# Starting the first batch by halves of its heads in a one-core attention and snake kernel

## The chip, the cores and the metric

One core of one Trainium2 chip runs the whole program. The metric is the device time of one execution in microseconds (us). Where the granted TensorE clock of an execution was below 0.997 of full speed, the text says so. PE is TensorE, ACT ScalarE, DVE VectorE, POOL GpSimd, SP SyncE.

## The reference

Attention without a score matrix, then a two-layer block with the snake activation. Eight batches, eight heads, 576 positions, 64 columns per head.

```python
q_s = softmax(q, over head_dim)            # exp, sum, divide
k_s = softmax(k, over seq)
kv  = einsum('bhsd,bhse->bhde', k_s, v)
x   = einsum('bhsd,bhde->bhse', q_s, kv)   # -> 4608 tokens x 512
h   = x @ w_in                             # 512 -> 2048
g   = h + sin(alpha * h)**2 / alpha
out = g @ w_out                            # 2048 -> 512
```

## The kernel before

Tokens go through the two products in nine rows of 512. A row has 16 blocks of h (128 of the 2048 columns each): four matmuls over the four k-chunks of x give a block, ACT takes its sine, one of ACT, DVE and POOL squares it, DVE combines (`g = h + s / alpha`), and PE multiplies g by w_out into four accumulators. Row t = 0 can't start until the first batch's q, k, v have been loaded, exponentiated, normalised and multiplied into x. "Half 0" and "half 1" below are the two halves of the heads: half 0 gives x chunks 0 and 1, half 1 gives chunks 2 and 3.

The kernel has eight PSUM banks at hand, and until the end of row 1 they are split in two pools:

```python
ps_h = tile_pool(name="ps_h", bufs=4, space=PSUM)      # single banks
ps_e = tile_pool(name="ps_e", bufs=2, space=PSUM)      # double banks, lent to h
...
def mm_h(t, ni, wide=None, k0=0, k1=4):                # one block of h
    ...
    elif wide and ni % 6 in ((2, 3) if t == 0 else (4, 5)):
        hp = wide()                                    # a lent buffer (named hh)
    else:
        hp = ps_h.tile([128, MF], F32, name="hp", tag="h")
    for ki in range(k0, k1):
        nc.tensor.matmul(hp, win[:, ki, ...], xT[:, ki, ...], start=(ki == 0), stop=(ki == 3))
```

The start, with GpSimd issuing the loads of v and of the weights, and all four x chunks made after both halves of kv:

```python
GP_CP(held, staged["q", 0][:, 0, 0, 0:1])              # waits for q, holds the issues below
for ii, j0, j1 in ((0, 0, 9), (1, 0, 5), (1, 5, 9)):
    GP.dma_start(... v ...)
for c0, c1 in ((0, 256), (256, 512), (512, 1024), (1024, 1536), (1536, 2048)):
    load_win(c0, c1)                                   # two transfers each, all four k-chunks
...
for ii in range(2):
    kv_mm(0, ii, ps_e, split=True)
    kv_norm(0, ii, ii + 1)
for c in range(4):
    xp = ps_h.tile([128, MF], F32, name="hp", tag="h")
    attn_chunk(0, c, 0, 8, xp)
    (ACT_CP, DVE_CP)[c % 2](xT[:, c, 0:MF], xp)
```

Row 0 and the start of its second product:

```python
for ni in range(nN):
    h_slot(0, ni, "DPAPPAPPAPPAPPAP"[ni], lag, lent)   # who squares: DVE, POOL, ACT
    flush(lag, 1)                                      # combine, one block behind
    if ni in late: late[ni]()
flush(lag, 0)
accs = [ps_h.tile([128, dm], F32, name="hp", tag="h") for _ in range(4)]
os = o_quad(0, accs, ...)                              # the first 8 alternate accumulators 0 and 1
take(os, 20)                                           # 20 of the 64 matmuls
```

The softmax here doesn't subtract the row's maximum and nothing guards it: scores larger than these inputs give would overflow.

## Time and profile before

| | before |
|---|---|
| median (3 runs) | 288.67 us (288.63 to 289.37) |
| span of the profiled run | 286.8 us |
| first q landed, its exp starts | 4.94 us |
| h stream of row 0 starts | 15.74 us |
| first sine | 17.73 us |
| combine of block 13 ends | 31.66 us |
| tenth o matmul | 31.72 us |
| h stream of row 1 starts | 47.23 us |

The prediction below shows the lines that carry its reading. The first is the stretch-by-stretch table, one microsecond each: stretch, length, then busy time and count for PE, PE's weight loads, DVE, ACT and POOL, then the granted clock, the share of the DMA engines, and GB/s.

### The profile page before, as it was taken

The numbers are of one execution on the slowest core, as the hardware profiler recorded it, in microseconds if no ns is written. First come the engines' busy times: TensorE is split into PE (matmuls) and PEld (weight loads), VectorE is DVE, ScalarE is ACT, GpSimd is POOL, SyncE is SP. The second block draws the span as 40 slices with busy tenths as digits, with TensorE's granted clock in tenths as the row PEclk, the third lists the DMA queues.
The fourth block names the chain that finished last, engine by engine and source line by source line (L and its number), as shares of the span: only waits on it lengthen the run. The fifth ranks groups of instructions, "written<-read, shape, count | busy, mean of one in ns | idle before, by whom it ended". The sixth has DMA issues, their size and how long they took to land.

```text
span 286.8 us, 4259 instructions
## 1 busy us (share of the span) xinstructions
PE 274.9 (96%) x1570; PEld 130.6 (46%) x1570; DVE 188.5 (66%) x281; ACT 226.6 (79%) x320; POOL 81.6 (28%) x77
## 2 busy tenths in 40 slices
PE   1899999999999999999999999999999999999994
PEld 0444454445454445444544454445444444444443
DVE  3867775899968668756775677757674555555412
ACT  4889756999489999899889988998877777777500
POOL 4859420674766571005300530032000000000000
PEclk9999999999999999999999999999999999999999
DMA  7999999946799957129910990116011111111142
GB/s 253 309 205 242 269 391 408 307 169 191 167 199 402 361 184 120 38 43 358 289 37 21 336 308 27 37 39 139 17 39 37 37 37 39 37 37 38 41 109 73
DMA packets 37381, 45.77 MB, mean 160 GB/s; under 512 B 15968, under 2 KB 20848, under 8 KB 37360
## 3 DMA queue, kind: packets, MB, share of 16 engines
q1 hardware_dynamic: 32032, 39.98, 46.3%
q0 software_dynamic: 5136, 5.38, 10.2%
q8 instruction: 12, 0.20, 0.3%
q10 hardware_dynamic: 192, 0.14, 0.2%
q14 instruction: 9, 0.07, 0.1%
HBM read 36.71 MB, written 9.44 MB: 161 GB/s over the span
## 4 chain that ended last, share of the span: by engine, by line
PE 84%; DMA 7%; DVE 5%; POOL 1%; ACT 1%; issue 1%; SPq 0%; POOLq 0%
PE hp L234 38%; PE op L254 35%; DMA st_v<-in_v_dram 4%; PE hh L234 3%; PE kvp L157 2%; PE xp L206 2%; DMA qT<-qn 2%; DMA st_q<-in_q_dram 1%; DVE qs L144 1%; PE op L532 1%; PE op L234 1%; ACT s L240 1%; DVE qn L146 1%; POOL qn L146 1%; POOL s L244 1%
## 5 line engine op out<-in xcount | busy, mean ns | idle before, releaser
L250 DVE SCALAR_TENSOR_TENSOR g<-s,inva_sb,hp 128x512 bf16<-128x512 f32 x130 | 96.1, 745 | 64.1 <-ACT s L242 54.2
L234 PE MATMUL hp<-xT,win 128*128 128x512 bf16 x520 | 129.7, 379 | 0.0
L254 PE MATMUL op<-wout,g 128*128 128x512 bf16 x496 | 124.2, 379 | 0.0
L240 ACT ACTIVATE s<-hp,alpha_sb 128x512 f32<-128x512 f32 x130 | 87.6, 682 | 25.4 <-PE hp L234 24.3
L234 PEld LDWEIGHTS <-win 128*128 128x128 bf16 x576 | 56.3, 98 | 67.4 <-issue 0.4
L254 PEld LDWEIGHTS <-g 128*128 128x128 bf16 x560 | 54.1, 98 | 61.7 <-issue 0.9
L242 ACT ACTIVATE s<-s 128x512 f32<-128x512 f32 x112 | 70.5, 630 | 3.5
L146 POOL TENSOR_TENSOR qn<-qe,qs 128x1152 bf16<-128x1152 bf16 x12 | 25.3, 2128 | 73.2 <-DVE qs L140 63.1
L244 POOL TENSOR_TENSOR s<-s 128x512 f32<-128x512 f32 x29 | 30.5, 1061 | 24.8 <-ACT s L240 24.3
L260 DVE COPY o<-op 128x512 f32<-128x512 f32 (+2 forms) x33 | 22.1, 669 | 9.6 <-PE op L254 7.1
L117 ACT ACTIVATE ke<-st_k 128x1152 bf16<-128x1152 f32 x16 | 17.9, 1151 | 4.8 <-DMA st_k<-in_k_dram 4.1
L117 ACT ACTIVATE qe<-st_q 128x1152 bf16<-128x1152 f32 x16 | 17.9, 1156 | 2.8 <-DMA st_q<-in_q_dram 2.8
L139 DVE TENSOR_REDUCE qs<-qe 128x36 f32<-128x2304 bf16 x5 | 12.8, 2553 | 8.7 <-ACT qe L117 8.6
L131 POOL CAST vb<-st_v 128x1152 bf16<-128x1152 f32 x12 | 13.6, 1162 | 10.4 <-DMA st_v<-in_v_dram 10.4
L254 PE MATMUL hp<-wout,g 128*128 128x512 bf16 x64 | 15.1, 379 | 0.0
L209 DVE CAST xT<-xp 128x512 bf16<-128x512 f32 (+1 forms) x18 | 13.4, 742 | 0.0
L117 ACT ACT_TABLE_LOAD x7 | 9.0, 1283 | 1.3 <-PEq L546 1.2
L157 PEld LDWEIGHTS <-ke 64*128 64x128 bf16 x288 | 8.2, 93 | 3.5 <-ACT s L242 1.3
L157 PE MATMUL kvp<-vb,ke 64*128 64x130 bf16 x288 | 9.7, 216 | 0.0
L234 PE MATMUL hh<-xT,win 128*128 128x512 bf16 x40 | 9.4, 379 | 0.0
L144 DVE TENSOR_REDUCE qs<-qe 128x18 f32<-128x1152 bf16 x6 | 8.0, 1329 | 2.1 <-ACT qe L117 2.1
L206 PE MATMUL xp<-qT,kbd 128*128 128x256 bf16 (+1 forms) x40 | 8.2, 286 | 0.4 <-DVE xT L209 0.3
(68 smaller groups left out, 117.9 us busy)
## 6 DMA issues: line engine op xcount, KB each, us to landing
out_dram<-o SPq DMA_DIRECT2D x70, 128.0 KB, 2.3
st_q<-in_q_dram SPq DMA_DIRECT2D x6, 1152.0 KB, 6.3
st_k<-in_k_dram SPq DMA_DIRECT2D x6, 1152.0 KB, 8.2
st_v<-in_v_dram SPq DMA_DIRECT2D x6, 1152.0 KB, 10.3
st_q<-in_q_dram SPq DMA_DIRECT2D x4, 576.0 KB, 5.5
st_k<-in_k_dram SPq DMA_DIRECT2D x4, 576.0 KB, 7.1
wout<-in_moe_w_out_dram POOLq DMA_DIRECT2D x4, 512.0 KB, 11.2
win<-in_moe_w_in_dram POOLq DMA_DIRECT2D x6, 256.0 KB, 7.1
```

The source lines that it names most:

```text
L117: nc.scalar.activation(dst[:, :, ii * 128:(ii + 1) * 128].rearrange("p j (x d) -> p x j d", x=2), src[:, ii::2], AX.Exp)
L131: engs[ii](vv[:, 2 * ii:2 * ii + 2, :, 0:D], staged["v", b][:, ii::2])
L146: engs[ii % len(engs)].tensor_tensor(qn[:, ii].rearrange("p j (x d) -> p j x d", x=2), qe[:, ii], part.unsqueeze(3).to_broadcast([128, J, ...
L157: nc.tensor.matmul(kvp[:, e, ii * 130:(ii + 1) * 130], ke[r, j, ii * 128:(ii + 1) * 128], vt[r, j, ii * 130:(ii + 1) * 130], start=(j == 0 ...
L206: nc.tensor.matmul(xp[:, e, 0:n], kt[:, e, ii], qT[:, ii, j0:j1, e * 64:(e + 1) * 64], start=True, stop=True)
L234: nc.tensor.matmul(hp, win[:, ki, ni * 128:(ni + 1) * 128], xT[:, ki, t * MF:(t + 1) * MF], start=(ki == 0), stop=(ki == 3))
L240: nc.scalar.activation(s, hp, AX.Sin, scale=alpha_sb[:, ni:ni + 1])
L242: nc.scalar.activation(s, s, AX.Square)
L244: nc.gpsimd.tensor_tensor(s, s, s, op=ALU.mult)
L250: nc.vector.scalar_tensor_tensor(G[t][:, ni], in0=s, scalar=inva_sb[:, ni:ni + 1], in1=hp, op0=ALU.mult, op1=ALU.add)
L254: nc.tensor.matmul(acc, G[t][:, ni, j * 128:(j + 1) * 128], wout[:, ni, :], start=(ni == 0), stop=(ni == nN - 1))
L260: eng(o[:, cols], acc)
```

## The change

The intent: don't wait for all of q, k, v before the first matmul of h. Half 0 is loaded and worked through first; while half 1 is still on its way, PE already runs k-chunks 0 and 1 of the first four blocks. To free ACT and DVE, GpSimd casts the v of half 0. The core of the diff:

```diff
-        elif wide and ni % 6 in ((2, 3) if t == 0 else (4, 5)):
+        elif wide and ni % 6 in (4, 5):
...
+    for n, t, ii in (("q", q, 0), ("k", k, 0), ("q", q, 1), ("v", v, 0)):
+        load0(nc.sync, n, t, ii)
...
+    load0(GP, "k", k, 1)
+    load0(GP, "v", v, 1, 0, 5)
+    load0(GP, "v", v, 1, 5, 9)
+    load_win(0, 512, slice(0, 2))          # k-chunks 0 and 1
+    cast_v0(0, 0, 9, GP_CP)
+    load_win(0, 512, slice(2, 4))          # k-chunks 2 and 3
+    for c0 in (512, 1024, 1536):
+        load_win(c0, c0 + 512)
...
+    for c in range(2):
+        x_chunk(c, ps_h.tile([128, MF], F32, name="hp", tag="h"), (ACT_CP, DVE_CP)[c])
+    kv_mm(0, 1, ps_e, split=True)
+    kv_norm(0, 1, 2)
...
+    for ni in range(4):
+        mm_h(0, ni, None, 0, 1)
+    xp = ps_e.tile([128, 2, MF], F32, name="xp", tag="a")
+    for e in range(2):
+        x_chunk(2 + e, xp[:, e], DVE_CP)   # matmul, cast, matmul, cast
+    for ni in range(4):
+        mm_h(0, ni, None, 1, 2)
+    for ni in range(3):
+        mm_h(0, ni, None, 2, 3)
...
-        take(os, 20)
+        take(os, 10)
+        tp = ps_e.tile([128, 2, 128], BF16, name="tp", tag="a")
+        for ii in range(2):
+            q_transpose_ii(0, ii, 8, 9, tp[:, ii:ii + 1])
+        ACT_CP(A["qT", 0][:, :, 8], tp)
+        take(os, 10)
```

The first hunk is there because the four blocks begun early need four single banks; it changes which blocks use the lent buffers, and so which blocks' banks the accumulators of row 0 take over.

More of the change, by code (lines that the diff above doesn't have):

```diff
@@ L102, in load_batch, with load_win @@
         load("v", v, b)
-    def load_win(c0, c1):
+    def load_win(c0, c1, ks=slice(0, 4)):
         n = slice(c0, c1)
         for x in range(2):
-            nc.gpsimd.dma_start(out=win[64 * x:64 * x + 64, :, n], in_=win_v[x][:, :, n])
+            nc.gpsimd.dma_start(out=win[64 * x:64 * x + 64, ks, n], in_=win_v[x][:, ks, n])
     def load_wout(c):
@@ L113, with exp_to @@
     A = {}
-    def exp_to(dst, src):
-        for ii in range(2):
+    def exp_to(dst, src, iis=range(2)):
+        for ii in iis:
             nc.scalar.activation(dst[:, :, ii * 128:(ii + 1) * 128].rearrange("p j (x d) -> p x j d", x=2),
@@ L122, in exp_q, with exp_half @@
         exp_to(A["qe", b], staged["q", b])
+    def exp_half(name, b, ii):
+        if ii == 0:
+            A[name + "e", b] = att2.tile([128, J, 4 * D], BF16, name=name + "e")
+        exp_to(A[name + "e", b], staged[name, b], (ii,))
     def exp_k(b):
@@ L268, with load0 @@
     V, GP = nc.vector, nc.gpsimd
-    load("q", q, 0, halves=True)
-    load("k", k, 0, halves=True)
+    for n in "qkv":
+        staged[n, 0] = stage.tile([128, 4, J, D], F32, name=f"st_{n}", tag="st")
+    def load0(eng, n, t, ii, j0=0, j1=J):
+        eng.dma_start(out=staged[n, 0][:, ii::2, j0:j1].rearrange("p i j d -> p i (j d)"),
+                      in_=src_view(t, 0)[:, ii::2, j0 * D:j1 * D])
+    for n, t, ii in (("q", q, 0), ("k", k, 0), ("q", q, 1), ("v", v, 0)):
+        load0(nc.sync, n, t, ii)
     nc.scalar.dma_start(out=alpha_rows, in_=moe_alpha.rearrange("(no ni) -> no ni", ni=128))
@@ L282 @@
     ps_e = ES.enter_context(tc.tile_pool(name="ps_e", bufs=2, space=PSUM, reuse_waits="tile"))
-    tps = [ps_h.tile([128, 8, 128], BF16, name="tp", tag="h") for _ in range(3)]
+    tp0 = ps_h.tile([128, 8, 128], BF16, name="tp", tag="h")
     warm = ps_h.tile([128, 4, 128], F32, name="warm", tag="h")
@@ L289, with cast_v0 @@
     nc.vector.reciprocal(inva_sb, alpha_sb)
+    def cast_v0(ii, j0, j1, eng):
+        vv = vb[0].rearrange("p j (i c) -> p i j c", i=4)
+        eng(vv[:, 2 * ii:2 * ii + 2, j0:j1, 0:D], staged["v", 0][:, ii::2, j0:j1])
     GP_CP(singles.tile([128, 1], F32, name="held"), staged["q", 0][:, 0, 0, 0:1])
-    staged["v", 0] = st = stage.tile([128, 4, J, D], F32, name="st_v", tag="st")
-    for ii, j0, j1 in ((0, 0, 9), (1, 0, 5), (1, 5, 9)):
-        GP.dma_start(out=st[:, ii::2, j0:j1].rearrange("p i j d -> p i (j d)"),
-                     in_=src_view(v, 0)[:, ii::2, j0 * D:j1 * D])
-    for c0, c1 in ((0, 256), (256, 512), (512, 1024), (1024, 1536), (1536, 2048)):
-        load_win(c0, c1)
+    load0(GP, "k", k, 1)
[6 more added lines that the diff above has]
+        load_win(c0, c0 + 512)
     for c in range(2):
         load_wout(c)
-    exp_q(0)
-    exp_k(0)
     def warm_up(n):
@@ L308, in warm_up @@
             nc.tensor.matmul(warm, identb, A["qe", 0][:, 0:4, 0:128], start=True, stop=True)
-    def cast_v0(ii, j0, j1, eng):
-        vv = vb[0].rearrange("p j (i c) -> p i j c", i=4)
-        eng(vv[:, 2 * ii:2 * ii + 2, j0:j1, 0:D], staged["v", 0][:, ii::2, j0:j1])
+    exp_half("q", 0, 0)
+    exp_half("k", 0, 0)
+    exp_half("q", 0, 1)
     warm_up(7)
@@ L317, with x_chunk @@
     q_tile(0)
-    q_transpose_ii(0, 0, 0, 8, tps[0])
-    ACT_CP(A["qT", 0][:, 0, 0:8], tps[0])
-    cast_v0(0, 0, 5, ACT_CP)
-    cast_v0(0, 5, 9, DVE_CP)
-    warm_up(6)
-    q_transpose_ii(0, 1, 0, 8, tps[1])
-    for ii in range(2):
-        q_transpose_ii(0, ii, 8, 9, tps[2][:, ii:ii + 1])
-    cast_v0(1, 0, 5, DVE_CP)
-    cast_v0(1, 5, 9, ACT_CP)
-    ACT_CP(A["qT", 0][:, 1, 0:8], tps[1])
-    ACT_CP(A["qT", 0][:, :, 8], tps[2][:, 0:2])
-    for ii in range(2):
-        kv_mm(0, ii, ps_e, split=True)
-        kv_norm(0, ii, ii + 1)
-    for c in range(4):
-        xp = ps_h.tile([128, MF], F32, name="hp", tag="h")
-        attn_chunk(0, c, 0, 8, xp)
-        (ACT_CP, DVE_CP)[c % 2](xT[:, c, 0:MF], xp)
-    nc.scalar.activation(zero, zero, AX.Sin)
+    q_transpose_ii(0, 0, 0, 8, tp0)
+    ACT_CP(A["qT", 0][:, 0, 0:8], tp0)
+    exp_half("k", 0, 1)
+    warm_up(2)
+    kv_mm(0, 0, ps_e, split=True)
+    warm_up(3)
+    kv_norm(0, 0, 1)
+    tp1 = ps_e.tile([128, 8, 128], BF16, name="tp", tag="a")
+    q_transpose_ii(0, 1, 0, 8, tp1)
+    cast_v0(1, 0, 5, ACT_CP)
+    cast_v0(1, 5, 9, DVE_CP)
+    def x_chunk(c, xp, eng):
+        attn_chunk(0, c, 0, 8, xp)
+        eng(xT[:, c, 0:MF], xp)
+    for c in range(2):
+        x_chunk(c, ps_h.tile([128, MF], F32, name="hp", tag="h"), (ACT_CP, DVE_CP)[c])
+    kv_mm(0, 1, ps_e, split=True)
+    kv_norm(0, 1, 2)
+    ACT_CP(A["qT", 0][:, 1, 0:8], tp1)
+    nc.scalar.activation(zero, zero, AX.Sin)
+    for ni in range(4):
[7 more added lines that the diff above has]
+        mm_h(0, ni, None, 2, 3)
     def h_slot(t, ni, sq, lag, wide=None):
-        hp = mm_h(t, ni, wide, 2 if t < 2 and ni < 2 else 0)
+        done = 3 if t == 0 and ni < 3 else 2 if (t, ni) == (0, 3) or t == 1 and ni < 2 else 0
+        hp = mm_h(t, ni, wide, done)
         lag.append((t, ni, hp, sine(t, ni, hp, sq)))
@@ L373 @@
                 10: lambda: load_wout(3), 13: lambda: load("k", k, 1, halves=True, gate=DVE_CP)}
-        for ki in range(2):
-            for ni in range(2):
-                mm_h(0, ni, lent, ki, ki + 1)
         for ni in range(nN):
```

## The prediction

> **What bounds the kernel now.** I read the page first. TensorE (PE) is busy for 96% of the span, and its two big groups, the first product (L234, "h") and the second (L254, "o"), are streams of 512-column matmuls. The columns are instruction group, count, then busy us and mean ns of one, then idle time before it.
>
> ```profile
> PE 274.9 (96%) x1570; PEld 130.6 (46%) x1570; DVE 188.5 (66%) x281; ACT 226.6 (79%) x320; POOL 81.6 (28%) x77
> ...
> L234 PE MATMUL hp<-xT,win 128*128 128x512 bf16 x520 | 129.7, 379 | 0.0
> L254 PE MATMUL op<-wout,g 128*128 128x512 bf16 x496 | 124.2, 379 | 0.0
> ```
>
> 379 ns is one matmul with its modelled end. The pace is in the chain of waits, where 16 of them take 3.45 us: 0.216 us each. Then I read busy time by stretch (us; busy us and instruction count per engine).
>
> ```profile
> 0.00:15.74 15.74, 8.10 (x73) 3.99 (x74) 9.96 (x23) 9.88 (x12) 10.36 (x22) 1.00 0.97 274
> 15.74:29.60 13.86, 13.86 (x65) 6.25 (x64) 10.22 (x17) 13.51 (x22) 10.01 (x11) 1.00 1.21 236
> ...
> 47.20:283.20 236.00, 235.49 (x1309) 111.79 (x1307) 154.58 (x219) 192.04 (x275) 56.79 (x42) 1.00 0.47 135
> ```
>
> In the first 15.74 us no matmul of the h stream runs. From then to 29.60 there are 64 of them (plus one cut off at the edge) and 64 x 0.216 = 13.8: no holes. After 47.20 only 0.5 us is idle. So PE is the bound from 15.74 on, and an earlier start pays only if PE is not stopped later. But the second row has ACT busy for 13.51 of 13.86 us too: block row t = 0 is almost as tight for ACT as for PE. The timeline shows how it starts:
>
> ```profile
> 15.29 0.61 PE L214 MATMUL hp<-qT,kbd 128*128 128x512 bf16 x2 [0.23 <-DVE kbd L170]
> ...
> 15.74 1.95 PE L234 MATMUL hp<-xT,win 128*128 128x512 bf16 x8
> ...
> 17.73 1.25 ACT L240 ACTIVATE s<-hp,alpha_sb 128x512 f32<-128x512 f32 x2
> ```
>
> and how it ends, in the window 29.2 to 33:
>
> ```profile
> 28.83 3.17 POOL L244 TENSOR_TENSOR s<-s 128x512 f32<-128x512 f32 x3
> ...
> 29.61 3.56 PE L254 MATMUL hp<-wout,g 128*128 128x512 bf16 x15
> ...
> 29.92 0.75 DVE L250 SCALAR_TENSOR_TENSOR g<-s,inva_sb,hp 128x512 bf16<-128x512 f32 x1 [0.40 <-POOL s L244]
> ...
> 30.91 1.28 ACT L117 ACT_TABLE_LOAD   x1
> 30.91 0.75 DVE L250 SCALAR_TENSOR_TENSOR g<-s,inva_sb,hp 128x512 bf16<-128x512 f32 x1
> 31.58 1.40 DVE L250 SCALAR_TENSOR_TENSOR g<-s,inva_sb,hh 128x512 bf16<-128x512 f32 x2
> 31.72 1.17 PEld L254 LDWEIGHTS <-g 128*128 128x128 bf16 x6 [0.29 <-issue]
> ```
>
> The reader is to see the combines (L250) of blocks 12, 13, then 14 and 15, at 29.92, 30.91, 31.58, well after PE has begun the o products at 29.61. The weight load stops until 31.72, just after combine 13 ends at 31.66. That is the tenth o matmul, the first into the fourth accumulator, and this accumulator reuses the buffer of h block 13. Today this costs 0.17 us (the tenth would have come at 29.61 + 9 x 0.216 = 31.55).
>
> **What the Trainium skill says.** "TensorE: Matmul & The Clock Gate", Back-to-back issue gap, gives N/2.4 + 2.5 ns for a warm stream: 216 ns at N = 512, as this trace has it. "PSUM — Partial Sum Buffer", The four PSUM rules, says that one matmul output fits one bank, and the Specifications there that there are 8: four single-bank buffers here and two double ones. So six h blocks can be open at once, and which block's buffer an accumulator inherits matters. "ScalarE: Activation LUTs", What ACT_TABLE_LOAD costs, has about 1283 ns for the load; the trace has 1.28 us. "TensorE: Matmul & The Clock Gate", Why this matters for your kernels, warns of PE-idle gaps over some 3 us, after which the clock falls to half. The first seven warm-up matmuls here are 0.43 us apart (3.02 us for 7) against 0.216 later, which agrees for a cold start; no gap after that is long enough to show it.
>
> **The change part by part.** *Start.* Loads keep their count and bytes, but k and v of half 0 come on the sync queue, k and v of half 1 on the POOL queue. VectorE's chain for q is unchanged, and ends at 10.78 + 1.36 = 12.15. Only then can it normalise kv of half 0: 0.19 + 0.28 + 0.29, with gaps done at 12.95. PE multiplies the x chunks 0 and 1 at 13.0; ACT casts one (0.58) by about 14.0, DVE the other (v cast of 0.42 first, then 0.68) by 14.3. The first POOL-queue transfer landed 6.0 us after its issue at 5.09, so k of half 1 is there at 11.1; its exp (1.16) and a v cast (0.74) on ACT end near 13.05, so kv of half 1 is multiplied by 14.05 and normalised at 15.1, after DVE is free. Chunks 2 and 3 are multiplied by 15.6 and both cast on DVE (0.68 each) by 16.95. PE fills in: four block matmuls of k-chunk 0 from about 14.3 (weights landing), four of chunk 1 and three of chunk 2 from 15.6 to 17.15, then chunk 3. GpSimd's cast of v (1.16, by 10.5) is beside the q chain. So twelve h matmuls are done at 17.36; before, twelve are done at 15.74 + 12 x 0.216 = 18.33. **PE leads by 0.97 us.**
>
> *What ACT does with it.* ACT's sine waits for a complete block. The first is now complete at about 17.4, so it starts near 17.5 instead of 17.73. From there ACT needs 18 instructions to reach sine 14 (17.73 to 28.96 before, 0.62 each, no idle worth naming), and POOL's squares follow it without idle from 23 on, so the combines move by only **-0.25 us**: combine 12 ends at 30.4, combine 13 at 31.4. Six buffers let PE run ahead: each h block finds its buffer free by 0.1 to 0.3 us, so PE ends the row at 17.36 + 52 x 0.216 = 28.6.
>
> *The accumulators.* This is where I expect the loss. Buffers rotate. Before, blocks 2, 3, 8, 9, 14 and 15 used the two lent buffers, and the four accumulators inherited blocks 10, 11, 12, 13. Now 4, 5, 10 and 11 are lent and the accumulators inherit **12, 13, 14, 15**. The instruction order of both kernels, with waits, has VectorE waits on the first use of all four. The order of o matmuls alternates accumulators 0 and 1 for eight matmuls. So the first waits for combine 12 (30.4) and the second for combine 13 (31.4); eight more and the tenth starts at 31.4 + 8 x 0.216 = 33.1, against 31.72 before: **+1.4 us**. (Blocks 14 and 15 are combined by 32.1 and 32.7, in time.) PE is idle for some 2.6 us out of 28.6 to 31.4.
>
> *The late transposes.* Two transposes and their copy move behind the tenth o matmul: about **+0.2 us** on PE. The copy also sits ahead of ACT's table load, which moves from 30.91 to about 34.1, so exp of the next q ends near 37.7 instead of 34.5. That is 3 us of delay, but the second normalised q of batch 1 then comes at about 41.7, and PE, itself 1.6 late, needs it at 41.4 + 0.5: just hidden.
>
> *Given back.* The kernel before has 0.3 us of PE idle at 44.92, waiting for kbd, as VectorE's cast of v came late (chain below). With PE late and v in place, this goes: **-0.3**.
>
> Sum: 1.4 + 0.2 - 0.3 = +1.3 in the span, and from 47.20 on everything shifts with PE. 288.67 + 1.3 = 290.0; for the chance of the rivals below I say 289.8.
>
> **The rivals.** *A. The start pays and nothing gives it back.* Then 0.97 less 0.2: 287.9. For it: PE is the bound nearly everywhere. Against: ACT's 13.51 of 13.86 us, and the reused buffers.
> *B. The next batch's v takes the place.* The chain of waits runs through it:
>
> ```profile
> 32.24 10.53 DMA st_v<-in_v_dram
> 42.79 0.76 DVE vb L131
> ```
>
> The transfers are busy without a hole from 3 us to here, the same bytes are ahead of this v in both kernels, so it would land at about 42.8 again however early PE comes. If the accumulators did not wait, PE would still stop there and keep only some 0.2 us: 288.5.
> *C. The wait is longer than I think.* If the weights for k-chunks 2 and 3, issued only after GpSimd's cast, land late, the first sine slips behind 17.73 and all after it; or the 2.8 us almost without matmuls halves the PE clock for a window. Each some +0.5 to +1.5: up to 291.
>
> **Range and chances.** I give the accumulator wait 3 in 4, with +0.9 to +1.7 in it, A and B together 1 in 6, C the rest. So 289.8, and 288.4 to 291.0 for 8 in 10. 2% is 5.8 us, which no path here reaches: faster 0.01, same 0.97, slower 0.02.
>
> **What would show it.** Right: the h stream begins about 14.3; the first sine about 17.5; PE stops before the first and second o matmuls, released by combines 12 and 13, the tenth starts at about 33; the table load at about 34; the idle before the chunk at 44.9 is gone. Wrong: the first sine far earlier, so that ACT and the combines gain as much as PE; or o matmuls dense from 28.6; or kv of batch 1 waiting for its v at 42.8 with PE idle before it.

## More of the kernel before

```profile
14.00:15.00 1.00, 0.60 (x4) 0.11 (x2) 0.91 (x5) 0.54 (x3) 1.00 (x3) 1.00 1.37 200
15.00:16.00 1.00, 0.77 (x4) 0.31 (x4) 0.97 (x3) 0.75 (x2) 1.00 (x2) 1.00 1.23 203
16.00:17.00 1.00, 1.00 (x6) 0.48 (x5) 0.63 (x1) 0.98 (x2) 0.36 (x1) 1.00 1.25 206
```

The last number is what to remember: while PE starts the h stream, the weights come in at 200 GB/s and more. The timeline of GpSimd has the reason: five of the transfers of w_in are issued back to back from 7.40 on.

```profile
7.40 3.13 POOL L107 DMA_DIRECT2D win<-in_moe_w_in_dram  x5
```

## The result, and the profile after

| | before | after |
|---|---|---|
| median (4 runs each, same rounds) | 288.97 us (288.63 to 289.37) | 291.86 us (291.5 to 292.24) |
| span of the profiled run | 286.8 us | 290.3 us |
| h stream of row 0 starts | 15.74 us | 14.48 us |
| first sine | 17.73 us | 19.45 us |
| combine of block 13 ends | 31.66 us | 33.54 us |
| tenth o matmul | 31.72 us | 35.32 us |
| h stream of row 1 starts | 47.23 us | 50.62 us |

The ratio is 1.010, with a 95% interval of 1.0077 to 1.0122. Ratios here compare the fast runs of the same rounds, so they are not quite the ratio of the medians quoted. The changed kernel is 1% slower, and outside the predicted range. Its h stream does start 1.26 us earlier, yet its first sine comes 1.72 us later. The stretches of the changed kernel, columns as above:

```profile
0.00:14.48 14.48, 8.62 (x67) 4.37 (x68) 8.77 (x19) 8.47 (x9) 9.08 (x19) 1.00 0.88 276
14.48:21.19 6.71, 4.55 (x21) 1.52 (x19) 3.37 (x8) 3.83 (x6) 3.18 (x6) 1.00 1.01 149
21.19:31.56 10.37, 10.37 (x48) 4.71 (x49) 8.44 (x14) 9.98 (x17) 9.08 (x10) 1.00 1.20 242
31.56:35.30 3.74, 2.25 (x10) 0.87 (x9) 2.94 (x6) 1.23 (x3) 2.24 (x3) 1.00 1.18 254
```

The kernel before has no hole in PE from 15.74 to 29.60. Here the second stretch has 2.16 us without PE (6.71 less 4.55), and the fourth 1.49 (3.74 less 2.25): two holes, one on each side of a dense row. The bytes fell too: 149 GB/s on average in the second stretch. By single microseconds:

```profile
14.00:15.00 1.00, 1.00 (x17) 0.54 (x12) 0.94 (x4) 1.00 (x2) 1.00 (x2) 1.00 0.61 83
15.00:16.00 1.00, 0.91 (x4) 0.14 (x3) 0.52 (x2) 0.98 (x2) 1.00 (x3) 1.00 0.58 58
16.00:17.00 1.00, 0.24 (x2) 0.12 (x2) 0.69 (x1) 0.59 (x2) 0.52 (x1) 1.00 0.89 98
```

58 to 98 GB/s, where the kernel before moved 200. The timeline of the start names both causes of the first hole:

```profile
9.57 1.16 POOL L307 CAST vb<-st_v 128x1152 bf16<-128x1152 f32 x1 [0.96 <-DMA st_v<-in_v_dram]
10.68 3.04 POOL L107 DMA_DIRECT2D win<-in_moe_w_in_dram  x5
...
14.48 1.04 PE L239 MATMUL hp<-xT,win 128*128 128x512 bf16 x4
15.59 0.39 PE L219 MATMUL xp<-qT,kbd 128*128 128x512 bf16 x1
16.01 0.69 DVE L349 CAST xT<-xp 128x512 bf16<-128x512 f32 x1 [0.48 <-PE xp L219]
16.76 0.38 PE L219 MATMUL xp<-qT,kbd 128*128 128x512 bf16 x1 [0.78 <-DVE xT L349]
18.39 1.89 PE L239 MATMUL hp<-xT,win 128*128 128x512 bf16 x8 [0.39 <-DMA win<-in_moe_w_in_dram]
19.45 1.84 ACT L245 ACTIVATE s<-hp,alpha_sb 128x512 f32<-128x512 f32 x3 [2.85 <-PE hp L239]
21.19 1.90 PE L239 MATMUL hh<-xT,win 128*128 128x512 bf16 x8 [0.92 <-DMA win<-in_moe_w_in_dram]
```

First, GpSimd waits 0.96 us for v and casts for 1.16, so the weights for k-chunks 2 and 3, next in its order, are issued only from 10.68. In the trace, the second of them lands at 18.25, and PE starts on k-chunk 2 at 18.39. Second, the two matmuls of x chunks 2 and 3 (L219) are 1.17 us apart. The second does not depend on the first for data; it waits for DVE's cast of the first (0.78 us in the bracket). Both write into one double buffer, and the buffer's second half is ordered behind the read of its first.

The chain of waits that ended last ran through q's transfer and DVE's normalisation of q in the kernel before. It now runs through GpSimd's cast and the weights:

```profile
9.57 1.16 POOL vb L307
...
12.46 8.69 DMA win<-in_moe_w_in_dram
...
27.17 0.73 POOL wout L110
27.91 2.04 POOL s L249 x2
```

Its last part, from 25.13 to the combine at 32.79, runs through GpSimd's squares and its two issues of w_out.

The end of row 0, in the window 31 to 36.5, answers to the lines of the kernel before around its 29.61:

```profile
32.59 0.38 PE L259 MATMUL hp<-wout,g 128*128 128x512 bf16 x1 [0.87 <-DVE g L255]
...
32.79 2.06 DVE L255 SCALAR_TENSOR_TENSOR g<-s,inva_sb,hp 128x512 bf16<-128x512 f32 x3
...
33.59 2.10 PE L259 MATMUL hp<-wout,g 128*128 128x512 bf16 x9 [0.62 <-DVE g L255]
...
35.84 0.37 ACT L416 COPY qT<-tp 128x256 bf16<-128x256 bf16 x1 [3.02 <-PE tp L191]
36.23 1.28 ACT L117 ACT_TABLE_LOAD   x1
```

The DVE line holds the combines of blocks 13, 14 and 15; the first takes 0.75 us and ends at 33.54. The first o matmul waits for the combine of block 12, the second for that of block 13: as predicted, but 2.2 us later than predicted. The copy of the late transposes stands ahead of ACT's table load, which moves from 30.91 to 36.23.

### The profile page after: what moved, and what is told of

The parts are those of the page before. It is cut to its first block, busy times and chain, and to the rows that moved or that the text cites. A ratio compares the mean times of both kernels' runs of the same rounds, so it can differ in the third digit from the quotient of the medians.

```text
span 290.3 us, 4257 instructions
## 1 busy us (share of the span) xinstructions
PE 276.6 (95%) x1569; PEld 131.0 (45%) x1569; DVE 189.0 (65%) x281; ACT 225.9 (78%) x318; POOL 82.5 (28%) x78
## 4 chain that ended last, share of the span: by engine, by line
PE 81%; DMA 7%; POOL 5%; ACT 2%; DVE 2%; issue 1%; SPq 0%; POOLq 0%
PE hp L239 34%; PE op L259 33%; PE hp L259 5%; DMA win<-in_moe_w_in_dram 3%; POOL s L249 3%; DMA st_v<-in_v_dram 2%; PE kvp L162 2%; PE hh L239 2%; ACT s L245 2%; PE xp L211 2%; DMA qT<-qn 2%; PE op L563 1%; PE op L239 1%; POOL qn L151 1%; POOL win L107 1%
## 5 line engine op out<-in xcount | busy, mean ns | idle before, releaser
L255 DVE SCALAR_TENSOR_TENSOR g<-s,inva_sb,hp 128x512 bf16<-128x512 f32 x132 | 97.5, 746 | 64.4 <-ACT s L247 54.2
L239 PE MATMUL hp<-xT,win 128*128 128x512 bf16 x528 | 131.8, 379 | 0.4 <-DMA win<-in_moe_w_in_dram 0.4
L245 ACT ACTIVATE s<-hp,alpha_sb 128x512 f32<-128x512 f32 x132 | 89.0, 682 | 28.3 <-PE hp L239 27.9
L136 POOL CAST vb<-st_v 128x1152 bf16<-128x1152 f32 x12 | 13.6, 1163 | 10.5 <-DMA st_v<-in_v_dram 10.5
L162 PE MATMUL kvp<-vb,ke 64*128 64x130 bf16 x288 | 10.4, 221 | 0.0
L239 PE MATMUL hh<-xT,win 128*128 128x512 bf16 x32 | 7.6, 379 | 0.9 <-DMA win<-in_moe_w_in_dram 0.9
```

The costliest lines, as they stand in the source:

```text
L136: engs[ii](vv[:, 2 * ii:2 * ii + 2, :, 0:D], staged["v", b][:, ii::2])
L162: nc.tensor.matmul(kvp[:, e, ii * 130:(ii + 1) * 130], ke[r, j, ii * 128:(ii + 1) * 128], vt[r, j, ii * 130:(ii + 1) * 130], start=(j == 0 ...
L239: nc.tensor.matmul(hp, win[:, ki, ni * 128:(ni + 1) * 128], xT[:, ki, t * MF:(t + 1) * MF], start=(ki == 0), stop=(ki == 3))
L245: nc.scalar.activation(s, hp, AX.Sin, scale=alpha_sb[:, ni:ni + 1])
L255: nc.vector.scalar_tensor_tensor(G[t][:, ni], in0=s, scalar=inva_sb[:, ni:ni + 1], in1=hp, op0=ALU.mult, op1=ALU.add)
```

## The experiments

Theory: the first sine is late from two causes, each partly hidden behind the other (weights issued late behind GpSimd's cast; x chunk 3 held by the read of chunk 2), and the rest of the loss is the accumulators' wait. Rivals: the transposes, a lower clock after PE's stop, v of batch 1, and POOL's squares setting the pace of row 0. Each edit is of the changed kernel unless it says "before"; the headings give the run's short name (e1 to e12), which the expectations use. The kernel before had medians of 289.0, 288.8 and 288.99 us in the three sets, 7, 7 and 9 runs. The third set (e9 to e12) ran on another chip than the first two. The second set has one run of it at 291.75, which widens the intervals there and lowers their ratios; medians are then the better guide. Every run's output was right.

When the first q lands differs from trace to trace by some 0.4 us, so an absolute time of one trace is compared with care, and where it matters I give the start of the matmul of x chunk 2 too.

### The cast taken from GpSimd (e1)

```diff
     exp_half("q", 0, 1)
+    cast_v0(0, 0, 9, ACT_CP)
...
-    cast_v0(0, 0, 9, GP_CP)
```

> The changed kernel with one edit: the first half's v is cast on ACT, so GpSimd issues its w_in transfers without a break. Theory H (the cast holds the issue of w_in, the transfers run dry, and the second pair of w_in pieces lands at 14.9 and 18.3 us): both land by about 15.5, the first sine comes at about 18.8 instead of 19.45 (then the second x chunk's wait for VectorE is what is left), the h matmuls no longer stop before 21.2, and the time falls by about 0.6 us, to 291.2. Rival S (the new shape of the pieces, two of four k-chunks by 512 columns, is what is slow): the second pair still lands after 17.5 and the time stays within 0.3 us of 291.86.

Median 292.15 us, ratio 1.0108 [1.0074, 1.0142]. The two runs at full clock took 291.14 and 291.55; the two at a mean clock of 0.994 took 292.75 each. In the profiled run (full clock) the transfers stay full: 204, 198 and 208 GB/s in the same three microseconds. PE no longer waits for weights, and the first sine is at 18.77. What is left in the waits of PE from 14 to 50 us (total, times, longest) is

```profile
PE hp L259 <- DVE g L255: 2.3, 2, 1.6
PE xp L219 <- DVE xT L349: 0.8, 1, 0.8
```

So the cast was the cause of the dry transfers. But the median does not fall to the 291.2 that I expected: PE stops for longer before the o products (2.3 us in place of 1.5), and two of the four executions have the lower mean clock.

### The weights issued first, the cast second (e2)

```diff
-    cast_v0(0, 0, 9, GP_CP)
     load_win(0, 512, slice(2, 4))
+    cast_v0(0, 0, 9, GP_CP)
```

> The changed kernel with one edit: GpSimd issues all four w_in pieces of columns 0 to 512 before it casts v. The cast stays on GpSimd and the shapes stay. Theory H: the second pair lands by about 15.5, the first sine at about 18.8, time about 291.2; the cast ends about 11, which PE does not feel as VectorE frees the norm of kv only at 12.3. Rival S: landing after 17.5 and 291.86. If the later pieces (columns 512 on) still land late with the cast between, the time is as in the changed kernel though the second pair is early.

Median 291.19 us, ratio 1.0089 [1.0055, 1.0123]; three runs at full clock of 290.92 to 291.37, one at 0.994 of 292.73. The transfers run at 165 to 194 GB/s, the weights of k-chunks 2 and 3 have landed by 15.5, and the first sine is at 18.58. From 14 us on it has the same two waits as the run before it (ahead of that, PE waits 1.2 us for GpSimd's cast, which now comes later). Compared with that run, GpSimd keeps its cast, so the place of the cast in GpSimd's order is the cause, not the cast itself.

### Both x chunks multiplied before either is cast (e4)

```diff
     for e in range(2):
-        x_chunk(2 + e, xp[:, e], DVE_CP)
+        attn_chunk(0, 2 + e, 0, 8, xp[:, e])
+    for e in range(2):
+        DVE_CP(xT[:, 2 + e, 0:MF], xp[:, e])
```

> The changed kernel with one edit: both x chunks of half 1 are multiplied before either is cast, so the second no longer waits for VectorE's read of the first in the same double buffer (0.96 us of PE). Theory: the two delays ahead of the first sine overlap. With the weights for k-chunk 2 still landing at about 18.2, the first sine stays at about 19.4 and the time within 0.3 us of 291.86. Rival (they add up): first sine about 18.5, time about 290.9.

Median 291.74 us, ratio 1.0092 [1.0036, 1.0147]. No gain. The first sine at 18.99 is 0.46 earlier than in the changed kernel, but only because the weights of k-chunk 2 happened to land 0.46 earlier in this trace (17.79 against 18.25; x chunk 2 was multiplied at 15.72 against 15.59). PE starts k-chunk 2 right behind them in both. It now reaches k-chunk 2 sooner and waits 0.74 us for its weights, against 0.39: the cause removed here was hidden behind the other.

### Both causes removed (e8)

> The changed kernel with two edits: w_in of columns 0 to 512 issued before GpSimd's cast, and both chunks multiplied before their casts. Theory: with both delays gone the first sine comes at about 17.6, as the prediction had it, and the combines about 1.8 us before those of the changed kernel; the accumulators' stop is still there (PE stands for about 2.6 us after the h row): time about 289.9, which is the predicted 289.8. Rival: the wait moves to batch 1's v, and under 1 us is gained.

The edits of the last two together. First sine 17.92:

```profile
16.11 1.29 DVE L363 CAST xT<-xp 128x512 bf16<-128x512 f32 x2 [0.81 <-PE xp L219]
...
17.92 1.84 ACT L245 ACTIVATE s<-hp,alpha_sb 128x512 f32<-128x512 f32 x3 [1.25 <-PE hp L239]
```

Yet the median is 291.94 us, ratio 1.0075 [1.0007, 1.0143]. The four executions split by clock: 290.31 at 1.0, and 292.04, 291.95, 291.92 at 0.994, 0.992, 0.992. The profiled one is of the second kind. Its stretch from 32 us (clock third from the end), and its o matmuls:

```profile
32.00:35.50 3.50, 3.50 (x9) 1.20 (x9) 1.21 (x2) 0.00 (x0) 0.22 (x1) 0.53 1.21 236
```
```profile
31.94 3.73 PE L259 MATMUL hp<-wout,g 128*128 128x512 bf16 x9 [0.62 <-DVE g L255]
```

Nine matmuls in 3.73 us: twice the 2.10 of the changed kernel. PE reaches the o products earlier, but the accumulators are free no earlier relative to the row; it stops 1.65 us, does one matmul, stops 0.62 more, and the granted clock of that stretch is 0.53: it is 0.50 from 31.86 to 35.27 and 1.00 on both sides. That eats the gain of both repairs. The stops alone don't decide it: the traces of e1 and e2 have the same two (1.64 and 0.62 us) at a clock of 1.00, and of those kernels' four executions two (e1) and one (e2) lost clock.

### The stop filled with matmuls that nobody reads (e10)

The kernel of the last run, and after the row's last combine is queued:

```diff
         flush(lag, 0)
+        fill = ps_e.tile([128, 4, 128], F32, name="fill", tag="a")
+        for _ in range(8):
+            nc.tensor.matmul(fill, identb, A["qe", 0][:, 0:4, 0:128], start=True, stop=True)
```

> e8 (weights first, chunks first) with eight more matmuls that nobody reads, put into PE's stop ahead of the o stream. In e8's trace PE stands for 2.8 us but for one matmul there, and then ten o matmuls come 0.43 us apart at a granted clock of 0.53. Theory C (the stop lets the clock fall, and that costs about 1.6 us): with the stop filled the clock stays 1.0, all executions are at about 290.3, the fastest of e8, and the extra work costs nothing. Rival: e8's 291.9 has another cause, and the eight matmuls add 0 to 1.7 us to it.

Median 290.17 us, all five at a clock of 0.998 or more; ratio 1.0039 [1.0025, 1.0054]. The same nine o matmuls:

```profile
31.77 2.10 PE L259 MATMUL hp<-wout,g 128*128 128x512 bf16 x9 [0.62 <-DVE g L255]
```

2.10 us in place of 3.73, and 1.77 us off the median by work that is thrown away. With e8's own split (290.31 against some 291.9) that shows the clock loss, and its size. That it was the fill that kept the clock is likely but not shown: this set ran on another chip, where no execution of any kernel fell below 0.997, and e8 was not run there. What stays over the kernel before, 1.2 us by medians, I put down to the accumulators' wait, still there in the line above.

### The accumulators' order, in both kernels (e3, e5)

In the changed kernel, other blocks use the lent buffers, so that the accumulators take over the banks of blocks 8, 11, 12 and 13, in this order, in place of 12 to 15:

```diff
-        elif wide and ni % 6 in (4, 5):
+        elif wide and (ni in (4, 5, 9, 10, 14, 15) if t == 0 else ni % 6 in (4, 5)):
```

> The changed kernel with one edit: blocks 4, 5, 9, 10, 14 and 15 take the lent double buffers, so that the four o accumulators inherit h blocks 8, 11, 12 and 13 instead of 12 to 15. Theory A (the accumulators' wait): the o stream starts at about 31.8 without the two stops of 1.0 and 0.8 us, the tenth o matmul comes at about 33.7 instead of 35.3, and the time falls by about 1.6 us, to 290.2. Rival (the stop is only moved, since ACT and POOL bound the row and the next waits take over): less than 0.5 us gained.

Median 291.0 us, ratio 1.0082 [1.005, 1.0114]: 0.86 better than the changed kernel (0.5 by the ratios), where I expected 1.6. The two stops are gone: ten o matmuls run densely from 30.94, and the tenth starts 0.05 after the combine of block 13 ends (32.83), in place of 1.78. Some of this is given back, to rival B, v of batch 1:

```profile
44.84 0.69 PE L162 MATMUL kvp<-vb,ke 64*128 64x130 bf16 x18 [0.41 <-ACT vb L136]
```

PE arrives earlier and waits 0.41 us for ACT's cast of v, which itself waited for the transfer; the transposes wait 0.3 for a combine. One of its four runs (291.92) had a clock of 0.994 that I have no trace of. Its start is that of the changed kernel, but in its trace v landed 0.5 us earlier, x chunk 2 was multiplied at 14.81, and the first sine is at 18.33: so the lateness of the weights varies by itself. Combine 13 too comes 0.71 earlier in it than in the changed kernel's, so the gain is not the buffers' alone.

And in the kernel before, the new order alone:

```diff
-        elif wide and ni % 6 in ((2, 3) if t == 0 else (4, 5)):
+        elif wide and ni % 6 in (4, 5):
```

> The kernel before with one edit: in block row 0 the lent buffers go to blocks 4, 5, 10, 11 as in the changed kernel, so the accumulators inherit 12 to 15. Nothing else of the change. Theory A: the first o matmul waits for combine 12, the second for combine 13 (31.66), the tenth comes at about 33.4 instead of 31.72, less 0.3 given back at the next batch: about +1.4 us, 290.3. Rival: other waits hide it, within 0.3 us of 288.9.

Median 289.65 us, ratio 1.0027 [1.0004, 1.0049], so +0.8 by the ratio; I expected 1.4. The mechanism is there:

```profile
30.45 0.38 PE L254 MATMUL hp<-wout,g 128*128 128x512 bf16 x1 [0.95 <-DVE g L250]
31.45 4.26 PE L254 MATMUL hp<-wout,g 128*128 128x512 bf16 x19 [0.62 <-DVE g L250]
```

The tenth o matmul is at 31.45 + 8 x 0.216 = 33.18, 1.46 later than before, although combine 13 ends 0.27 earlier in this trace (31.39). So it comes 1.79 after combine 13, against 0.06 before: 1.73 for the buffers. PE ends 0.93 later than in the trace of before: half a microsecond of the 1.46 is given back, 0.3 of it at batch 1's waits.

### A held issue put into the kernel before (e6)

```diff
-    for c0, c1 in ((0, 256), (256, 512), (512, 1024), (1024, 1536), (1536, 2048)):
+    load_win(0, 256)
+    GP_CP(singles.tile([128, 2, J, D], BF16, name="held_k"), staged["k", 0][:, 1::2])
+    for c0, c1 in ((256, 512), (512, 1024), (1024, 1536), (1536, 2048)):
         load_win(c0, c1)
```

> The kernel before with one edit: GpSimd makes an unused copy of k's second half (1.16 us, it can start at 9.2) after the first two w_in pieces, as long a hold as the changed kernel's cast. Theory H: the fourth piece lands after 17 instead of at 15.3 and the later ones 1 to 2 us later, PE stops before the third and fifth h block, and the time rises by 0.5 to 1.3 us. Rival: the transfers that are queued cover the hold, the landings move by under 0.5 us and the time stays within 0.3.

Median 290.91 us, 2.1 over the before of its set; ratio 1.0059 [1.0007, 1.0111], lowered by that one slow run of before. The same dry stretch appears:

```profile
15.00:16.00 1.00, 0.63 (x4) 0.31 (x4) 0.96 (x3) 0.88 (x3) 1.00 (x2) 1.00 0.92 80
```

80 GB/s in place of 203, and PE stops 1.2 us for w_in. (With a wait for k ahead of the copy, GpSimd issues nothing from 8.25 to 10.63.) So a cast between GpSimd's issues dries the transfers without the rest of the change. It cost more than I had expected: the fifth piece too is late, at 19.39 (before: 16.52), which makes the tenth o matmul 1.4 late, and after it PE waits 0.3 us for w_out and 0.7 for batch 1's v.

### All three repaired (e7)

> The two edits of e8 and the accumulators of e3 (blocks 4, 5, 9, 10, 14, 15 in the lent buffers). Theory: all three waits gone, no stop at the o stream; against e8 another -0.6 to -1.6 us, as some is given back where batch 1's v or its k arrives: 288.3 to 289.3, so about as fast as the kernel before. Rival: 288.0 or less if the 0.97 us lead of PE came through.

The weights issued first, both x chunks multiplied first, and the order of buffers of the first of the two kernels above. Median 289.17 us, 288.91 to 289.5, ratio 0.9999 [0.9948, 1.005] (against the medians, 0.4 over). The three parts together take back nearly all of the 2.9 us, and no more. Where PE's lead goes is seen in row 0:

```profile
23.92 1.89 PE L239 MATMUL hh<-xT,win 128*128 128x512 bf16 x8 [0.89 <-DVE g L255]
```

PE waits in the middle of the row for a combine to free a bank. The first sine is at 17.88, no earlier than before, and the combines follow it at the old distance.

### Three more attempts at a gain, and all miss (e9, e11, e12)

On top of the last kernel, the transposes four o matmuls later and their copy on DVE, so that ACT's table load is not behind them:

```diff
-        take(os, 10)
+        take(os, 14)
...
-        ACT_CP(A["qT", 0][:, :, 8], tp)
-        take(os, 10)
+        DVE_CP(A["qT", 0][:, :, 8], tp)
+        take(os, 6)
```

> e7 (weights first, chunks first, old accumulators) with the two late transposes four o matmuls later and copied by VectorE instead of ACT. Theory: the 0.44 us wait of the transposes for combine 14 goes, ACT's table load comes right after the last sine, at about 31.3 instead of 33.3; time 0.3 to 0.6 us under e7's 289.17, so about 288.7. Rival: hidden both times, 289.1.

Median 288.99 us, ratio 1.0012 [0.9992, 1.0033]. The table load is back at 31.25 and the wait of the transposes is gone, but the median is only 0.2 below the last kernel's (in another set, on another chip), within the noise, and equal to that of the kernel before in its own set. Then the square of block 11 moved from ACT to DVE, on top of this kernel and alone in the kernel before:

```diff
-            h_slot(0, ni, "DPAPPAPPAPPAPPAP"[ni], lag, lent)
+            h_slot(0, ni, "DPAPPAPPAPPDPPAP"[ni], lag, lent)
```

> e9 with one of ACT's five squares of row 0 (block 11) on VectorE. Theory (ACT, POOL and VectorE bound row 0, so PE's lead is of no use until they are faster): the last combines come 0.3 to 0.6 us earlier and the time falls by as much, to about 288.3. Rival: VectorE has no room (0.75 us for each of 16 combines in a row of 13.9 us), and the time stays or rises by up to 0.5.

> The kernel before with the same square on VectorE, the control for e11. PE is dense in row 0 there, so the theory says no change, within 0.3 us of the kernel before; if it gains as much as e11 does over e9, the gain has nothing to do with the change.

Medians 289.36 (ratio 1.0015 [0.9998, 1.0032]) and 289.48 us (1.0031 [0.9998, 1.0064]). No gain in either: taking one square from ACT does not free row 0. From the first sine to the end of combine 13 it takes 13.97 us with the move and without it. These runs relieve ACT; none takes a square or an issue from GpSimd, through which the chain of waits above runs, so GpSimd as the limit of row 0 is left untested. No kernel beats the one before.

## Why the prediction was wrong

**The failed step is "What ACT does with it".** It said that the first sine starts near 17.5 and that the combines move by -0.25 us. The first sine came at 19.45 and the combine of block 13 moved by +1.88. The rest of the step held: not PE but the work behind the sines sets the pace of row 0. From first sine to the end of combine 13 are 13.93 us before (17.73 to 31.66) and 14.09 after (19.45 to 33.54). In the nine other traces in which PE doesn't stop for weights after the first sine it is 13.94 to 13.97, and in the three others in which it does, 14.10 to 15.26. So a late first sine is paid in full, and the dense h stream behind it can't help. Whether it is ACT or POOL that sets this pace is not shown. The 1.95 us between 17.5 and 19.45, all with x chunk 2 multiplied near 15.5:

- 0.42: with both causes removed, the first sine is still at 17.92. The prediction let DVE cast chunks 2 and 3 from 15.6 to 16.95; in that run kv of half 1 is normalised at 15.30 (I had 15.1), the two matmuls start at 15.48, and DVE starts at 16.11 and ends at 17.40. I had given the normalisation 0.2 us too little and the two matmuls some 0.3.
- 0.85: from there to the 18.77 of the run without GpSimd's cast: x chunk 3 held by the cast of chunk 2. This wait stood in the instruction order that I had read, and I counted it nowhere.
- 0.68: from there to 19.45, the late weights (0.13 of it is a later start of the chunk). Rival C named this, at +0.5 to +1.5, and I gave it what was left of the chances, 1 in 12.

This split holds in this order only: with the late weights still there, removing the chunk's wait alone gave nothing.

**Of the start, only the first matmuls were right.** The h stream began at 14.48 (I said about 14.3), GpSimd's cast ended at 10.73 (10.5). But the lead of 0.97 us after twelve h matmuls was not there: held up by the same two waits, the twelfth starts at 19.03, against 18.17 before. With both waits removed (e8) it starts at 17.50.

**The accumulators were right, in mechanism and in size.** PE stops before the first and second o matmul for combines 12 and 13. The tenth starts at 33.59 + 8 x 0.216 = 35.32, which is 3.60 later than before: 1.88 for the late row and 1.72 for the buffers. My 1.4 had the row's -0.25 in it, so for the buffers it meant 1.65 or so; in the kernel before (e5) they measure 1.73. Undone alone this part gave 0.86, and done alone it cost 0.8: what it costs at the end is less than in place, since part is given back at batch 1.

**The late transposes** cost 0.1 in the chain (I had 0.2). The table load came at 36.23 (34.1), late with the row, and still hidden. **Given back** 0.3: the idle before the chunk at 44.9 is gone, as predicted.

Sum: 1.88 + 1.72 + 0.1 - 0.3 = 3.4 us. The h stream of row 1 starts 3.39 later, and PE ends 3.5 later in the traces; the medians differ by 2.9. The prediction's sum was 1.3, and the missing 2.1 are the row's -0.25, hidden in its 1.4, that was +1.88.

**The rivals.** A fell: even with everything repaired no gain is left, and PE waits in row 0 for a combine. B is real, but shows only when the accumulators don't wait. Of C, the weights are in the result; the lower clock is not (all four runs at 0.998 or more), though it lies just behind: with the start alone repaired (e8), it takes 1.6 us from three of four executions (some 291.9 against 290.31 at full clock).

**What stays open.** Why the transfers need some 3 us to fill again after a hold of some 2 us, though from 10.68 on the pieces are issued every 0.6 us. The runs show that the hold causes it, not how. Nor is it shown what sets the 13.97 us from the first sine to combine 13: in the chain of waits it is GpSimd's squares and issues, and no run made these shorter. What decides whether a stop of PE costs clock is open too.

## What to carry to other kernels

An earlier start pays only if the engine that sets the pace of the next stage starts earlier: follow the change up to the first instruction of that engine (here ACT's first sine), not to the first matmul. A queue that issues transfers is a resource like any other, so work that waits for data should stand behind the issues that others need soon, not between them. When two causes overlap, undoing one can show little or nothing; undo each, then both, and look at the clock before judging the sum.

## What the Trainium skill lacked or had wrong

- "TensorE: Matmul & The Clock Gate", Why this matters for your kernels, puts the limit at PE-idle gaps of some 3 us. Here the clock was at 0.50 for 3.41 us after waits of 1.65 and 0.62 us with a single matmul between them, in the trace of one execution (e8); three of that kernel's four had a mean clock of 0.992 to 0.994. Waits of 0.87 and 0.62 us left it at 1.00 in the changed kernel, but so did 1.64 and 0.62 in the traces of e1 and e2: the length of the waits is not all that decides. A lone matmul did not save the clock in e8, and the page doesn't say how much work in a gap does; with eight in it, five executions (e10, on another chip) stayed at 0.998 or more.
- "DMA: Bandwidth & Descriptors", Anatomy of one DMA — SWDGE (gpsimd) path, fits a transfer as 2.0 us and its bytes over 436e3 per us. A piece of w_in of 128 KB would take 2.3 us by this, one of 256 KB 2.6 (estimates from the page). The medians from issue to landing were 5.9 and 7.1 us in the kernel before, 6.3 and 9.6 in the changed one: the fit, given per DMA, does not hold for transfers that queue behind each other. It has no word on a queue refilling after a hold; here the rate was 58 to 98 GB/s for three microseconds, against some 200 without the hold.
- No page that I read says that a second matmul into the other bank of one double PSUM buffer can be ordered behind the read of the first; it is the program's own ordering, and put the second matmul 1.17 us behind the first, where two multiplied together are 0.2 apart.
